# Attention with an expert layer: the large loads on ACT's queue, POOL's weight operations one period later

## The chip, the cores and the metric

The kernel runs on one core of a Trainium2 chip. The metric is device time in microseconds (us), the median of three runs; the times below, where nothing else is said, come from one execution that the hardware profiler recorded. The engines are TensorE (PE in the profile; PEld is its weight load), VectorE (DVE), ScalarE (ACT), GpSimd (POOL) and SyncE (SP). SP and ACT can each issue transfers (DMAs), and each has a queue of its own, which 16 DMA engines work off.

## The reference

Linear attention with exponential features over 8 batches and 8 heads, 576 positions of 64 numbers each, and then a two-layer expert network on the joined heads:

```python
def phi(x):
    proj = np.einsum('bhsd,df->bhsf', x, w_phi)              # 128 features
    proj = proj - np.max(np.abs(proj), axis=-1, keepdims=True)
    return np.concatenate([np.exp(proj), np.exp(-proj)], axis=-1)
q_p, k_p = phi(q), phi(k)
kv  = np.einsum('bhsf,bhsd->bhfd', k_p, v)
z   = np.sum(k_p, axis=2)
num = np.einsum('bhsf,bhfd->bhsd', q_p, kv)
den = np.einsum('bhsf,bhf->bhs', q_p, z)[..., None] + 1e-06
x   = (num / den) joined over heads                          # 4608 x 512
h   = x @ w_in                                               # w_in 512 x 2048
out = (h - np.tanh(h)) @ w_out                               # w_out 2048 x 512
```

The two expert weights arrive as 64-bit floats.

## The kernel before, in words

The work has two stages. The attention stage goes through 32 units, each a pair of heads of one batch, as a software pipeline: `ramp` starts the first three, `period(i)` for i from 3 to 31 works on six units at once, each at another step, and `drain` ends the last. The expert stage (`head`, `frame`, `finish`) then runs 48 frames of matmuls that take 7 products where a plain 2 x 2 block product takes 8. The order on each engine is the order in which the code is written; nothing is rescheduled. Each engine works its list in order and waits on semaphores for others.

In period i the names stand for units: `a` is unit i, `c` is i-1, `p` is i-2, `r` is i-3, `q` is i-4, `o` is i-5. A period does this:

- `project(a)`: PE projects the unit's queries and keys (tile `qk`) onto the features, into `pj`, `pa`, `pt`. `centre` on DVE finds the largest size in each row (`m`) and subtracts it (`t`). `k_exp` and `q_exp` on ACT take the exponentials (`kp`, `qe`).
- `kadd(c)`: POOL adds the key features of five blocks in four additions (L419 to L422) into `ss`. One period later `ksum` (L428) on PE sums `ss` over partitions, and `ksum_copy` (L432) on ACT copies the feature sums to `kst`.
- `denom(r)` on PE (L470) and `denom_copy` on ACT (L487) make the denominators `dd`. Then a chain of small transfers: `den_recip_load` (L492) gathers `dd` into `dn`; DVE takes the reciprocal `rn` (L497), ahead of the next period's `centre`; `den_store` (L502) writes it to memory as `rr`; in the next period `den_spread` (L507) reads it back spread over partitions as `rb`; in the period after that `den_mul` (L510) on POOL multiplies the attention output `d` with it, and `x_store` (L513) writes `d` to memory as `xs`.
- `kv` (L409), its copy, its transposition and `num` (L456) on PE make the numerators.
- Beside the attention, one tile of an expert weight per period is converted from 64 to 32 bits: `dec_load` (L267, L272) loads it raw (`rawi`, `rawo`), `dec_0` on ACT (L279) and three steps on DVE (L283 to L291) convert it. The converted tiles of `w_in` are combined in pairs for the 7 products: `Prep.steps` gives subtractions on POOL (L168, tiles `s` and the low parts of `wr`) and casts on ACT (L185, the high parts of `wr`). The table `aside` says in which period which of these run: `aside[i][0]` on ACT, `aside[i][1]` on POOL, `aside[i][2]` stores of finished pieces (`wd`, L112), `aside[i][3]` loads for the expert stage. A cast `h2` or `h4` stands one period after the POOL operation whose result it reads.
- `load(units[i+2])` (L303) fetches the queries and keys of the unit two periods on, 576 KB; `load_v` (L307) the values.

All loads and stores are issued by SP, except the first load of `w_phi`. On SP an instruction that waits holds up what is behind it.

Of the kernel before, what the change touches and what calls it, by code (L numbers as in the profile page):

```python
# [33 lines left out]
def tile_linear_attention_moe(  # L34
# [10 lines left out]
    nc = tc.nc  # L45
# [181 lines left out]
    with ExitStack() as c1:  # L227
# [32 lines left out]
        def dec_load(n, queue=nc.sync):  # L260
            u = Dec()
            kind, u.f = tiles[n]
            u.nm = f"{kind}{u.f}"
            u.d = wi if kind == "i" else wo
            u.r = raw.tile([P, DM], U64, tag="raw", name=f"raw{u.nm}")
            if kind == "i":
                queue.dma_start(  # L267
                    u.r.rearrange("p (c f) -> p c f", f=P),
                    w_in[:, u.f * P : (u.f + 1) * P].rearrange("(c p) f -> p c f", p=P),
                )  # L270
            else:
                queue.dma_start(u.r, w_out[u.f * P : (u.f + 1) * P, :])  # L272
            return u
# [26 lines left out]
        def load(u, queue=nc.sync):  # L300
            u.qk = pq.tile([P, PC], F32, tag="qk", name=f"qk{u.i}")
            for o, w in ((0, PC),) if u.i else ((5 * P, PC), (0, 5 * P)):
                queue.dma_start(u.qk[:, o:w], qkT[u.i][:, o:w])  # L303

        def load_v(u):
            u.v = pq.tile([P, 5, 2, D], F32, tag="v", name=f"v{u.i}")
            nc.sync.dma_start(u.v.rearrange("p j e d -> p (j e d)"), v5[u.i])  # L307


        def project(u, parts):  # L310
            for part in parts:
                if u.t is None:
                    u.t = [pq.tile([P, 2, 5, F], F32, tag="t0", name=f"t{u.i}_0"), None]
                    u.m = [p2.tile([P, 2, 5], F32, tag="m0", name=f"m{u.i}_0"), p2.tile([P, 2, 4], F32, tag="m1", name=f"m{u.i}_1")]
                if part == "j":
                    u.pj = ps_pj.tile([P, 2, 512], F32, tag="pj", name=f"pj{u.i}")
                    bank, tiles = u.pj, range(4)
                elif part == "t":
                    u.pt = ps_t.tile([P, 2, 512], F32, tag="pt", name=f"pt{u.i}")
                    bank, tiles = u.pt, range(4, 5)  # L320
                else:
                    u.pa = ps_d.tile([P, 2, 512], F32, tag="po", name=f"pa{u.i}")
                    bank, tiles = u.pa, range(5, 9)
                for k, a in enumerate(tiles):
                    for e in range(2):
                        hs = slice(e * D, (e + 1) * D)
                        nc.tensor.matmul(  # L327
                            bank[:, e, k * F : (k + 1) * F], u.qk[hs, a * P : (a + 1) * P], wph[hs, :], start=True, stop=True
                        )
# [10 lines left out]
        def centre(u, parts, h=None):  # L340
            for part in parts:
                x, m, t = part_of(u, part)
                if h is not None:
                    x, m, t = x[:, :, h], m[:, :, h], t[:, :, h]
                nc.vector.tensor_reduce(m, x, AX.X, ALU.max, apply_absolute_value=True)  # L345
                nc.vector.tensor_tensor(t, x, m.unsqueeze(3).broadcast_to(list(t.shape)), ALU.subtract)  # L346
# [48 lines left out]
        def k_exp(u, r, signs=(0, 1)):  # L395
            h, x, j = ((slice(SR, P), 4, 0), (slice(0, P), slice(0, 4), slice(1, 5)))[r]
            for s in signs:
                nc.scalar.activation(u.kp[h, :, j, s, :], u.t[r][h, :, x, :], AF.Exp, scale=1.0 - 2.0 * s)  # L398
# [18 lines left out]
        def kadd(u):  # L417
            x = p2.tile([P, 2, 2, F], F32, tag="ss", name=f"ss{u.i}")
            nc.gpsimd.tensor_tensor(x, u.kp[:, :, 1], u.kp[:, :, 2], ALU.add)  # L419
            nc.gpsimd.tensor_tensor(x, x, u.kp[:, :, 3], ALU.add)  # L420
            nc.gpsimd.tensor_tensor(x, x, u.kp[:, :, 4], ALU.add)
            nc.gpsimd.tensor_tensor(x, x, u.kp[:, :, 0], ALU.add)  # L422
            u.ss = x

        def ksum(u, x):
            u.pu = x
            for n in range(4):
                nc.tensor.matmul(x[n * 32 : (n + 1) * 32], ones, u.ss[:, n // 2, n % 2, :], start=True, stop=True)  # L428

        def ksum_copy(u):  # L430
            u.kst = p1.tile([P, F], F32, tag="kst", name=f"kst{u.i}")
            nc.scalar.copy(u.kst, u.pu)  # L432
# [31 lines left out]
        def denom(u, pu):  # L464
            u.pd = pu[:, F : F + CH]
            for s in range(2):
                for e in range(2):
                    for c in range(2):
                        n, w = 2 * e + c, 2 * e + s
                        nc.tensor.matmul(  # L470
                            u.pd[n * 32 : (n + 1) * 32, :],
                            u.ks[:, w * 32 : (w + 1) * 32],
                            u.qe[:, e, s, c * CH : (c + 1) * CH],
                            start=(s == 0),
                            stop=(s == 1),
                        )

        def num_copy(u):
            if u.i % 4 or u.i >= NU - 3:
                u.d = tail.tile([P, S], F32, tag="d", name=f"d{u.i}", bufs=3)  # L480
            else:
                u.d = p1.tile([P, S], F32, tag="d0", name=f"d{u.i}")
            nc.scalar.copy(u.d.rearrange("p (c n) -> p c n", c=2), u.po[:, :, 0:CH])  # L483

        def denom_copy(u):
            u.dd = pd.tile([P, CH], F32, tag="dd", name=f"dd{u.i}")
            nc.scalar.activation(u.dd, u.pd, AF.Identity, bias=bias_t[:, 3:4])  # L487

        def den_recip_load(u):
            w = 2 * S // P  # L490
            u.dn = tail.tile([P, w], F32, tag="dn", name=f"dn{u.i}")
            nc.sync.dma_start(u.dn, u.dd.rearrange("(n r) c -> n r c", r=32)[:, 0, :])  # L492
# [11 lines left out]
        def den_spread(u):  # L504
            u.rb = tail.tile([P, S], F32, tag="rb", name=f"rb{u.i}", bufs=1)
            for e in range(2):
                nc.sync.dma_start(u.rb[e * D : (e + 1) * D, :], u.rr[e : e + 1, :].broadcast_to([D, S]))  # L507

        def den_mul(u, pin=lambda ins: ins):
            pin(nc.gpsimd.tensor_tensor(u.d, u.d, u.rb, ALU.mult))  # L510

        def x_store(u):
            nc.sync.dma_start(xs[u.b // 2][u.hp, :, (u.b % 2) * S : (u.b % 2 + 1) * S], u.d)  # L513

        units = []
# [5 lines left out]
        NU = len(units)  # L521
# [7 lines left out]
        dec = []  # L529

        def unit(i):
            return units[i] if 0 <= i < NU else None

        def bank():
            return ps_c.tile([P, 512], F32, tag="pu", name="pu")
# [67 lines left out]
        def aside_at(i, late):  # L603
            for f in aside[i][late]:
                f()
# [56 lines left out]
        def period(i):  # L662
            a, c, p, r, q, o = (unit(i - n) for n in range(6))
            w = dec[i - 3]
            dec.append(dec_load(i - 2))
            if i > 3:
                num_copy(r)
            k_exp(c, 1)
            if o:
                den_mul(o)  # L670
                x_store(o)
            if i + 2 < NU:
                load(units[i + 2])
            project(a, "jat")
            centre(a, "jt")
            kadd(c)
            ksum(p, p.pc[:, 0:F])
            ksum_copy(p)
            pu = bank()
            denom(r, pu)  # L680
            denom_copy(r)
            den_recip_load(r)
            if q:
                den_spread(q)
            if i > 3:
                load_v(a)
            aside_at(i, 2)
            aside_at(i, 3)
            kv_turn(p)
            ksum_turn(p, p.pc[:, F : 2 * F])  # L690
            kv_turn_copy(p, nc.scalar.copy)
            ksum_turn_copy(p)
            dec_0(w, a.pt)
            if i < NU - 1:
                aside_at(i, False)
            aside_at(i, True)
            q_turn(c)
            q_turn_rest(c, pu)
            q_exp(c)
            q_exp_rest(c)  # L700
            centre(a, "a")
            k_exp(a, 0)
            kv(c)
            kv_copy(c)
            dec_1(w)
            dec_2(w)
            dec_3(w)
            if r:
                den_recip(r)
                den_store(r)  # L710
            num(p)
# [96 lines left out]
        for i in range(3, NU):  # L808
            period(i)
# [541 lines left out]
```

## Time and profile before

| | |
|---|---|
| three runs, median | 1057.58 us (1056.92 to 1059.92) |
| profiled execution, its own time | 1059.23 us |
| its span | 1057.4 us |
| PE busy | 1042.4 us (99%) |
| DVE busy | 870.2 us (82%) |
| ACT busy | 792.1 us (75%) |
| POOL busy | 272.8 us (26%) |
| bytes moved | 184.59 MB, 175 GB/s in the mean |

How to read it: PE counts as busy while any of its matmuls is under way, and their ends are modelled. A busy share over the whole span mixes the two stages: POOL has nearly all its work in the first 307 us. The granted clock of TensorE is full in all of both stages. The view by stretch tells the stages apart, the list of waits says who waited for whom, the chain follows the work that ended last, and the timeline shows when each instruction ran.

### The profile page before, as it was taken

The page shows a single profiled execution, that of the slowest core. Times are in us where ns is not written, and L with a number is a line of the kernel's source. Part 1 is how long each engine was busy: PE and PEld are TensorE (multiplying, and loading weights), DVE is VectorE, ACT ScalarE, POOL GpSimd, SP SyncE. Part 2 cuts the span into 40 slices and gives each one's busy share as a digit, 9 for nine tenths or more (in the row PEclk, how much of TensorE's full clock was granted, in tenths as well). Part 3 has the DMA queues.
Part 4 walks back from the last instruction along what each step waited for, and adds up shares of the span by engine and source line. Part 5 has one row for each costly group of instructions (what it writes and reads, how often), then busy time and mean ns, then how long its engine had stood idle before and what let it go on. Part 6 is the DMA issues. An engine that isn't in the chain of part 4 may idle for free.

```text
span 1057.4 us, 19349 instructions
## 1 busy us (share of the span) xinstructions
PE 1042.4 (99%) x7484; PEld 874.0 (83%) x7484; DVE 870.2 (82%) x1086; ACT 792.1 (75%) x1281; POOL 272.8 (26%) x233
## 2 busy tenths in 40 slices
PE   8999999999989999999999999999999999999998
PEld 6666666666668998999999999999999999999997
DVE  7899888889979899878887788867887778877776
ACT  5888888988878778766777666776677667776665
POOL 4799899989960000000000000000000000000000
PEclk9999999999999999999999999999999999999999
DMA  5789999999847653464335433345334543353311
GB/s 166 205 233 282 264 271 288 267 272 270 253 142 263 201 187 103 159 216 144 121 120 190 167 131 122 120 169 179 128 106 156 199 137 113 120 180 109 123 47 60
DMA packets 75738, 184.59 MB, mean 175 GB/s; under 512 B 15744, under 2 KB 30464, under 8 KB 75648
## 3 DMA queue, kind: packets, MB, share of 16 engines
q1 hardware_dynamic: 75360, 183.17, 53.9%
q8 instruction: 59, 0.97, 0.4%
q14 instruction: 31, 0.25, 0.1%
q10 hardware_dynamic: 288, 0.20, 0.1%
HBM read 149.49 MB, written 33.70 MB: 173 GB/s over the span
## 4 chain that ended last, share of the span: by engine, by line
PE 82%; DMA 7%; DVE 5%; ACT 2%; POOL 2%; issue 1%; SPq 1%; ACTq 0%; DVEq 0%; POOLq 0%
PE A L142 18%; PE B L142 14%; PE po L987 12%; PE po L988 12%; PE po L993 12%; DMA dn<-dd 4%; PE po L456 3%; PE pc L409 3%; DVE t L346 2%; PE pj L327 2%; PE pa L327 2%; PE pu L470 2%; DVE m L345 1%; DMA rb<-rr 1%; DMA rr<-rn 1%
## 5 line engine op out<-in xcount | busy, mean ns | idle before, releaser
L142 PE MATMUL A<-xo,wr 128*128 128x384 f32 x1152 | 231.5, 337 | 0.0
L142 PEld LDWEIGHTS A<-xo,wr 128*128 128x128 f32 x1152 | 204.9, 188 | 11.4 <-ACT d L483 0.5
L911 ACT COPY u<-A 128x384 f32<-128x384 f32 x143 | 68.5, 479 | 142.6 <-PE A L142 142.2
L142 PE MATMUL B<-xo,wr 128*128 128x384 f32 x864 | 173.7, 337 | 0.0
L142 PEld LDWEIGHTS B<-xo,wr 128*128 128x128 f32 x864 | 152.5, 188 | 4.2 <-DVE hx L918 0.4
L987 PE MATMUL po<-who,ghx 128*128 128x512 f32 x288 | 112.3, 390 | 0.7 <-ACT hy L925 0.7
L987 PE MATMUL po<-who,ghy 128*128 128x512 f32 x288 | 112.3, 390 | 0.3 <-ACT ghy L962 0.3
L988 PE MATMUL po<-wlo,ghx 128*128 128x512 f32 x288 | 112.0, 389 | 0.0
L988 PE MATMUL po<-wlo,ghy 128*128 128x512 f32 x288 | 112.0, 389 | 0.0
L510 POOL TENSOR_TENSOR d<-d,rb 128x576 f32<-128x576 f32 x32 | 46.3, 1448 | 165.4 <-DMA rb<-rr 160.8
L950 DVE SCALAR_TENSOR_TENSOR s2y<-s2y,thy 128x768 f32<-128x768 f32 x48 | 46.0, 959 | 51.5 <-ACT thy L941 51.5
L398 ACT ACTIVATE kp<-t 64x256 f32<-64x256 f32 (+1 forms) x126 | 85.1, 722 | 2.1 <-DVE t L346 1.0
L993 PE MATMUL po<-who,glx 128*128 128x512 f32 x288 | 80.9, 389 | 0.0
L935 ACT ACTIVATE yx<-hx 128x768 f32<-128x768 f32 (+1 forms) x49 | 41.0, 836 | 52.9 <-DVE hx L918 52.9
L993 PE MATMUL po<-who,gly 128*128 128x512 f32 x282 | 79.3, 389 | 0.3 <-DVE gly L965 0.3
L409 PE MATMUL pc<-kp,v 128*64 128x256 f32 x640 | 76.1, 384 | 0.5 <-DMA v<-in_v 0.4
L456 PE MATMUL po<-qe,kv 128*64 128x288 f32 x512 | 69.0, 412 | 0.4
L993 PEld LDWEIGHTS po<-who,glx 128*128 128x128 f32 x288 | 54.0, 188 | 11.2
L947 DVE SCALAR_TENSOR_TENSOR s2x<-s2x,yx 128x768 f32<-128x768 f32 (+1 forms) x49 | 46.1, 941 | 20.4 <-ACT s2x L936 19.1
L993 PEld LDWEIGHTS po<-who,gly 128*128 128x128 f32 x282 | 52.8, 188 | 11.7 <-DVE gly L965 0.8
L987 PEld LDWEIGHTS po<-who,ghx 128*128 128x128 f32 x288 | 54.1, 188 | 8.8 <-ACT hy L925 1.1
L987 PEld LDWEIGHTS po<-who,ghy 128*128 128x128 f32 x288 | 54.1, 188 | 8.5 <-ACT ghy L962 0.7
(186 smaller groups left out, 2228.8 us busy)
## 6 DMA issues: line engine op xcount, KB each, us to landing
wr<-wd SPq DMA_DIRECT2D x92, 512.0 KB
wr<-wd SPq DMA_DIRECT2D x46, 768.0 KB
qk<-in_qkT SPq DMA_DIRECT2D x31, 576.0 KB
v<-in_v SPq DMA_DIRECT2D x32, 320.0 KB
rb<-rr SPq DMA_DIRECT2D x64, 144.0 KB
xs<-d SPq DMA_DIRECT2D x32, 288.0 KB
out<-o SPq DMA_DIRECT2D x35, 256.0 KB
rawi<-in_moe_w_in SPq DMA_DIRECT2D x16, 512.0 KB
```

The costliest lines, as they stand in the source:

```text
L142: nc.tensor.matmul(bank[:, 0:HT], w[:, a, n, cs], x[:, b, c, :], start=start and i == 0, stop=i == 5, skip_group_check=not start,)
L327: nc.tensor.matmul(bank[:, e, k * F : (k + 1) * F], u.qk[hs, a * P : (a + 1) * P], wph[hs, :], start=True, stop=True)
L398: nc.scalar.activation(u.kp[h, :, j, s, :], u.t[r][h, :, x, :], AF.Exp, scale=1.0 - 2.0 * s)
L409: nc.tensor.matmul(u.pc[e * D : (e + 1) * D, 0 : 2 * F], u.v[:, j, e, :], u.kp[:, e, j, :, :], start=(j == first), stop=(j == last))
L456: nc.tensor.matmul(u.po[e * D : (e + 1) * D, c, 0:CH], u.kv[:, s, e * D : (e + 1) * D], u.qe[:, e, s, c * CH : (c + 1) * CH], start=(s == ...
L510: pin(nc.gpsimd.tensor_tensor(u.d, u.d, u.rb, ALU.mult))
L911: nc.scalar.copy(t, A[q][:, 0:HT])
L947: nc.vector.scalar_tensor_tensor(z.s[:, s], z.s[:, s], GC, z.y[:, s], ALU.add, ALU.mult)
L950: nc.vector.scalar_tensor_tensor(z.s[:, s], z.s[:, s], GK, z.th[:, s], ALU.mult, ALU.mult)
L987: nc.tensor.matmul(po, z.gh[:, ts], wh, start=first, stop=False)
L988: nc.tensor.matmul(po, z.gh[:, ts], wl, start=False, stop=False)
L993: nc.tensor.matmul(po, z.gl[:, ts], wh, start=False, stop=last)
```

## The change

Two things move, in `period` alone.

First, the raw weight load and the load of queries and keys are issued by ACT (`nc.scalar`) and stand behind `ksum_copy`; before, SP issued both, the first at the start of a period, the second behind `x_store`. Second, POOL does the weight operations of period i-1 in period i, between `den_mul` and `kadd`; before, it did those of period i at the end of period i, behind `kadd`. The last two periods keep their own weight operations at the end as well (there these are sums for the expert stage).

```diff
         def period(i):
             a, c, p, r, q, o = (unit(i - n) for n in range(6))
             w = dec[i - 3]
-            dec.append(dec_load(i - 2))
             if i > 3:
                 num_copy(r)
             k_exp(c, 1)
             if o:
                 den_mul(o)
                 x_store(o)
-            if i + 2 < NU:
-                load(units[i + 2])
+            if i <= NU - 2:
+                aside_at(i - 1, True)
             project(a, "jat")
             centre(a, "jt")
             kadd(c)
             ksum(p, p.pc[:, 0:F])
             ksum_copy(p)
+            dec.append(dec_load(i - 2, nc.scalar))
+            if i + 2 < NU:
+                load(units[i + 2], nc.scalar)
             pu = bank()
             denom(r, pu)
...
             if i < NU - 1:
                 aside_at(i, False)
-            aside_at(i, True)
+            if i >= NU - 2:
+                aside_at(i, True)
```

The next pieces show period 20, the one that starts at 182.14 us in the trace of the kernel before. On SP before, one period's transfers from the reciprocals' store on (`rawi` is a raw weight tile, `qk` the queries and keys of unit 22):

```order
L502 DMA rr_2765<-rn_2763 128x9
L267 DMA rawi_2776<-in_moe_w_in 128x4x128
L513 DMA xs_89<-d_2496 128x576
L303 DMA qk_2784<-in_qkT 128x1152
L492 DMA dn_2836<-dd_2834 128x1x9
L507 DMA rb_2838<-rr_2765 64x576 x2
L307 DMA v_2841<-in_v 128x640
L112 DMA wd_4_109<-wr_2_2430 128x512
L112 DMA wd_0_107<-wr_0_2571 128x512
```

The same on SP after:

```order
L502 DMA rr_2760<-rn_2758 128x9
L513 DMA xs_89<-d_2492 128x576
L492 DMA dn_2836<-dd_2834 128x1x9
L507 DMA rb_2838<-rr_2760 64x576 x2
L307 DMA v_2841<-in_v 128x640
L112 DMA wd_4_109<-wr_2_2430 128x512
L112 DMA wd_0_107<-wr_0_2571 128x512
```

The two large loads are gone from SP: the store of `xs` follows that of `rr`, and the gathering of `dn` follows `xs`. On ACT before, from the last exponentials to the first cast of a weight pair (`kst` are the feature sums, `dd` the denominators, `wr_1` the cast):

```order
L398 ACTIVATE kp_154<-t_1_2740 128x2x4x128 x2
L432 COPY kst_2823<-pc_2745 128x128
L487 ACTIVATE dd_2834<-pu,bias_t 128x288
L449 COPY kv_2848<-pc_2745 128x256
L441 COPY ks_2850<-pc_2745 128x128
L279 ACTIVATE pt_2807<-rawo_2635 128x512
L185 CAST wr_1_2853<-s_3_2711 128x512
```

The same on ACT after:

```order
L398 ACTIVATE kp_154<-t_1_2735 128x2x4x128 x2
L432 COPY kst_2819<-pc_2740 128x128
L267 DMA rawi_2821<-in_moe_w_in 128x4x128
L303 DMA qk_2823<-in_qkT 128x1152
L487 ACTIVATE dd_2834<-pu,bias_t 128x288
L449 COPY kv_2848<-pc_2740 128x256
L441 COPY ks_2850<-pc_2740 128x128
L279 ACTIVATE pt_2803<-rawo_2680 128x512
L185 CAST wr_1_2853<-s_3_2777 128x512
```

The two loads stand between the copy of the feature sums and that of the denominators. On POOL before, from the weight operations of period 19 (`s_3`, `s_4`) to those of period 20, with the multiplication `d` and the four additions `ss`:

```order
L168 TENSOR_TENSOR s_3_2711<-wi_2337 128x256
L168 TENSOR_TENSOR s_4_2712<-wi_2198,wi_2337 128x256
L168 TENSOR_TENSOR s_3_2711<-s_3_2711,wi_2198 128x256
L510 TENSOR_TENSOR d_2496<-d_2496,rb_2697 128x576
L419 TENSOR_TENSOR ss_2814<-kp_154 128x512
L420 TENSOR_TENSOR ss_2814<-ss_2814,kp_154 128x512
L421 TENSOR_TENSOR ss_2814<-ss_2814,kp_154 128x512
L422 TENSOR_TENSOR ss_2814<-ss_2814,kp_154 128x512
L168 TENSOR_TENSOR s_4_2712<-wi_2198,s_3_2711 128x256
L168 TENSOR_TENSOR wr_1_2853<-s_3_2711,wr_1_2853 128x512
```

The same on POOL after:

```order
L510 TENSOR_TENSOR d_2492<-d_2492,rb_2697 128x576
L168 TENSOR_TENSOR s_3_2777<-wi_2334 128x256
L168 TENSOR_TENSOR s_4_2778<-wi_2194,wi_2334 128x256
L168 TENSOR_TENSOR s_3_2777<-s_3_2777,wi_2194 128x256
L419 TENSOR_TENSOR ss_2810<-kp_154 128x512
L420 TENSOR_TENSOR ss_2810<-ss_2810,kp_154 128x512
L421 TENSOR_TENSOR ss_2810<-ss_2810,kp_154 128x512
L422 TENSOR_TENSOR ss_2810<-ss_2810,kp_154 128x512
L510 TENSOR_TENSOR d_2633<-d_2633,rb_2838 128x576
```

The three operations of period 19 have moved behind the multiplication of period 20 and ahead of its additions; the cast `wr_1` on ACT, which reads `s_3`, has kept its place in period 20.

## Rows read from the trace of the kernel before

**Rows 1.** By stretch: length, busy us (instructions) PE, PEld, DVE, ACT, POOL, clock, DMA, GB/s

```profile
42.12:284.19 242.07, 238.81 (x3044) 160.44 (x3043) 217.69 (x287) 212.69 (x418) 219.54 (x186) 1.00 0.90 264
284.19:306.60 22.41, 19.69 (x234) 11.95 (x232) 17.38 (x25) 17.44 (x32) 21.86 (x16) 1.00 0.58 191
340.00:1050.00 710.00, 710.00 (x3576) 644.04 (x3574) 569.22 (x688) 502.74 (x719) 6.06 (x3) 1.00 0.41 140
```

**Rows 2.** Timeline of period 20: start, us, engine, line, operation, tiles, [idle before]

```profile
182.14 1.16 PE L327 MATMUL pj<-wph,qk 64*128 64x128 f32 x16
...
183.00 0.75 POOL L168 TENSOR_TENSOR s<-s,wi 128x256 f32<-128x256 f32 x1
...
183.36 0.38 SPq L267 DMA_DIRECT2D rawi<-in_moe_w_in  x1
...
184.66 1.42 POOL L510 TENSOR_TENSOR d<-d,rb 128x576 f32<-128x576 f32 x1 [0.92 <-PE pt L327]
184.89 0.27 ACT L432 COPY kst<-pc 128x128 f32<-128x128 f32 x1
...
185.86 0.50 ACT L487 ACTIVATE dd<-pu,bias_t 128x288 f32<-128x288 f32 x1 [0.70 <-PE pu L470]
...
186.11 0.32 SPq L513 DMA_DIRECT2D xs<-d  x1
...
186.52 0.39 SPq L303 DMA_DIRECT2D qk<-in_qkT  x1
...
186.58 0.27 ACT L441 COPY ks<-pc 128x128 f32<-128x128 f32 x1
...
186.91 2.38 PE L409 MATMUL pc<-kp,v 128*64 128x256 f32 x20
187.00 0.59 SPq L492 DMA_DIRECT2D dn<-dd  x1
187.31 0.62 ACT L185 CAST wr<-s 128x512 fp32r<-128x512 f32 x1
...
187.69 1.14 SPq L507 DMA_DIRECT2D rb<-rr  x2
...
190.16 1.29 POOL L422 TENSOR_TENSOR ss<-ss,kp 128x512 f32<-128x512 f32 x1
...
191.23 1.16 PE L327 MATMUL pj<-wph,qk 64*128 64x128 f32 x16
...
193.44 0.43 PE L428 MATMUL pc<-ss,ones 128*32 128x128 f32 x8
```

**Rows 3.** Who waited for whom, 42.12 to 284.19 us: total, times, longest

```profile
POOL d L510 <- DMA rb<-rr: 11.7, 16, 1.8
...
DVE rn L497 <- DMA dn<-dd: 9.1, 11, 1.3
```

**Rows 4.** Chain that ended last, followed from 236 us: start, us, what

```profile
215.29 5.69 DMA dn<-dd
```

**Rows 5.** DMA queues, 2.5 to 3.3 us (q1 SP's, q10 ACT's): packets, MB, share

```profile
q1 hardware_dynamic: 118, 0.23, 73.9%
q10 hardware_dynamic: 122, 0.06, 29.9%
```

**Rows 6.** By stretch, POOL's weight operations (L168) alone

```profile
42.12:284.19 242.07, 51.34 (x56) 1.00 0.90 264
```

**Rows 7.** Timeline of POOL, the multiplications' first, latest and last

```profile
42.97 1.41 POOL L510 TENSOR_TENSOR d<-d,rb 128x576 f32<-128x576 f32 x1 [1.66 <-DMA rb<-rr]
...
212.97 1.41 POOL L510 TENSOR_TENSOR d<-d,rb 128x576 f32<-128x576 f32 x1 [1.75 <-DMA rb<-rr]
...
275.76 1.27 POOL L168 TENSOR_TENSOR wr<-wi,wr 128x512 fp32r<-128x512 f32 x1
277.68 1.41 POOL L510 TENSOR_TENSOR d<-d,rb 128x576 f32<-128x576 f32 x1 [0.65 <-DMA rb<-rr]
```

**Rows 8.** Line of the denominators' copy: ACT's sequencer waiting, ns least/median/most

```profile
L487 ACTq EVENT_SEMAPHORE  x31: 616/895/2111, 35.8 to 308.5; - x31
```

## The prediction

> **What bounds the kernel now.** I read the busy time by stretch first [rows 1]. In the expert stage, from 340 to 1050 us, TensorE has work all the time, and the change does not reach it. What can move is the attention stage: 26 whole periods from 42.12 to 284.19 us, and its end up to 306.6 us. A period with no stall lasts 9.09 us: the first projection of one starts at 182.14 us and of the next at 191.23 [rows 2]. The 26 periods took 242.07 us [rows 1], 9.31 each, so stalls cost them 242.07 - 26 x 9.09 = 5.7 us. That is the prize, 0.54% of the run.
>
> Next, who waits. DVE waited 11 times, 9.1 us in all, for `dn`, the gathered denominators, and POOL 16 times, 11.7 us, for `rb`, the spread reciprocals [rows 3]. The chain shows what the first does: `dn` is 5.69 us from issue to landing [rows 4]; the reciprocal follows on DVE, and in its order the row maxima of the next projection queue behind it. Both loads are small and stand behind large ones on SP's queue. In the period at 182 us [rows 2] the order is raw weight (183.36), `xs` (186.11, it waits for POOL's multiplication that began at 184.66 and took 1.42), `qk` (186.52), `dn` (187.00), `rb` (187.69). So there is a loop: multiplication, `xs`, `qk`, `dn`, `rb`, and the next period's multiplication.
>
> **The change part by part.** Times are sums against the profiled execution's 1059.23 us, which is its span of 1057.4 and 1.8 around it; the median of the three timed runs is 1057.58, and I move that by the same sum.
>
> (a) SP loses the two large loads. `dn` is issued 0.48 us after `qk` began to be issued [rows 2], and that goes out of the loop, so `dn` and `rb` start 0.48 earlier. Whether they also land sooner after their issue is open, since the same bytes still move at the same time, now from another queue. The DVE waits labelled with `dn` come to 9.1 us in 11 [rows 3]; 0.48 off each is 5.3, or 58%. I take the same share of the 5.7 us of stalls: -3.3. Bounds: 0 (the bytes in front are the same) and -5.7 (all stalls go).
>
> To set row against rule: during 0.8 us at the start both queues had work, and the engines took 118 packets (0.23 MB) from SP's and 122 (0.06 MB) from ACT's [rows 5]. They alternate one packet for one, whatever its size. The Trainium skill, page "DMA: Bandwidth & Descriptors", section "Queues, rings and completion order", says the same, and under "Issuing engines are not separate DMA queues" that a second issuing engine only saves the first one's issue time. By that rule the 0.48 is all there is, and (a) stays at -3.3; without it, small loads that overtake would give the whole -5.7. The row sides with the rule: a 2304-byte row of `rb` then alternates with a 4608-byte row of `qk`.
>
> (b) POOL puts the weight operations between the multiplication and the additions. They take 51.34 us in the 26 periods, 1.97 each [rows 6]. Now the additions end at 190.16 + 1.29 = 191.45, and TensorE wants them for the feature sums at 193.44: 1.99 us to spare, with a multiplication that began 2.52 into its period [rows 2]. With 1.97 more ahead of them the spare is 0.02. So from now on every delay of `rb` past that point is TensorE's. POOL waited 11.7 us for `rb` [rows 3], at the worst 1.75 us, ahead of the multiplication at 212.97 [rows 7]. Of the 26 multiplications the first starts at 42.97, 0.85 us into its period, the last at 277.68, 2.58 into the one that began at 284.19 - 9.09 = 275.10 [rows 1, 7]; read one by one they lie 0.84 to 3.54 us in, 2.68 in the mean. If none moves, the excess over 2.54 sums to 9 us; if all move forward by the 0.48 of (a), to 3. Some of that is the same lateness that (a) leaves, since a TensorE that waits here no longer waits there, so I take +2.1, with 0 and +9 as the ends.
>
> (c) ACT gets two issues a period behind the copy of the feature sums (184.89), ahead of the denominators' copy (185.86) [rows 2]. The cover is the wait for TensorE there: ACT's sequencer stood in it 895 ns in the median, 616 at the least [rows 8]. On SP the issues took 0.38 and 0.39 us, and the next began 0.41 to 0.48 after the last [rows 2]: about 0.95 for both. That is 0.05 over the median cover and 0.33 over the least. Queued behind is the chain denominators, `kv`, `ks`, and the first matmul after `ks` starts at 186.91, while `ks` ends at 186.58 + 0.27 = 186.85 [rows 2]: 0.06 of slack. So mostly nothing shows; I take 0.03 x 26 = +0.8. Bounds: 0 (ACT only gets work) and 0.33 x 26 = +8.6. No row shows a load's issue on ACT in this stage. The raw load starts 1.7 us later than now but is wanted a period later; `qk` is wanted two periods later, so the landings are covered.
>
> (d) One cast on ACT per even weight pair (187.31 in the period shown) reads what the third of POOL's weight operations wrote, at 183.00 for 0.75 us [rows 2]. Now all three come behind the multiplication: 184.66 - 0.48 + 1.42 + 3 x 0.75 = 187.85, so the cast waits 0.5. There are four such pairs; the exponentials behind it are wanted by TensorE only later, so I take half of 2.0: +1.0. Bounds 0, and 4 x 1.0 = +4 where `rb` is not earlier and the whole wait reaches TensorE.
>
> (e) At the end POOL bounds: from 284.19 to 306.60 it is busy for 21.86 of 22.41 us, and TensorE for 19.69 [rows 1]. The last weight operation (275.76, 1.27 us) ran ahead of the multiplication at 277.68, which then still waited 0.65 for `rb` [rows 7]; now it follows that multiplication. With `rb` 0.48 earlier the end moves by 1.27 - 0.48 = +0.8; bounds -0.65 (the wait goes) and +1.27.
>
> Sum: -3.3 + 2.1 + 0.8 + 1.0 + 0.8 = +1.4 us, so 1060.6 for the profiled execution and 1057.58 + 1.4 = 1059.0 for the median. The gain in one wait comes back as others.
>
> **Rivals.** First, faster: the small loads do overtake the large ones. For it: with fewer bytes ahead in their own queue `rb` need only beat 2.54 us into the period, and then POOL's multiplication can follow the additions at once. Against: one-for-one alternation [rows 5]. It gives -5.7 from (a), 0 from (b) and (d), +0.8 from (c) and 0 from (e): 1052.7.
>
> Second, slower: POOL's order decides. Place: the feature sums at 193.44 waiting for the additions. It decides once `rb` lands as late as now, so that the multiplication begins over 2.54 us into most periods. Price: (b) at +9, against which the whole wait of DVE is hidden (-5.7), with (c) +0.8, (d) +1 and (e) +1.3: +6.4, 1064.0. For it: the mean start of 2.68 is already past the point. Against: 0.48 of issue gone.
>
> Third, the loads do not fit on ACT: (c) at its upper end, +8.6 instead of +0.8, on the forecast's other terms: 1066.8. For it: 0.95 against 0.616 of cover; against: the median of 0.895.
>
> **How the numbers follow.** A measurement of this kernel tells 0.3%, 3.2 us, from no change, so faster means under 1054.4 and slower over 1060.8. Forecast 0.50, its own range 1055.5 to 1061.5, of which 0.42 lies within the bound and 0.08 above. First rival 0.25; second 0.19; third 0.06. Faster 0.25, same 0.42, slower 0.33. The range reaches to the first rival and past the second: 1052.5 to 1065.5, leaving out the third and the tail of the first.
>
> **What would show it.** Right: periods of about 9.25 us, fewer DVE waits for `dn`, a new wait of TensorE's feature sums for POOL's additions, the cast of (d) waiting for POOL, and the denominators' copy on ACT starting within 0.1 us of where it does. Wrong: multiplications that start under 1.5 us into the period (first rival); feature sums that wait over 0.3 us in most periods (second); the denominators' copy 0.3 us later in most periods (third). A larger wait in the expert stage would contradict all of it.

## The result, and the profile after

The changed kernel takes 1071.18 us (median of 4 runs, 1069.65 to 1072.38) against 1058.21 for the kernel before on the same chip: ratio 1.0121, 95% interval 1.0099 to 1.0143. It is slower by some 13 us, outside the range of the prediction and above all its rivals. The profiled execution took 1070.35 us, with a span of 1068.6.

First, where the 11.2 us of span lie. The table by stretch of the changed kernel answers to [rows 1] (length, busy us of PE, PEld, DVE, ACT, POOL, granted clock, DMA share, GB/s); the stretches are the same 26 periods, the end of the stage, and the expert stage:

```profile
42.80:294.90 252.10, 241.05 (x3046) 161.89 (x3044) 217.86 (x287) 211.05 (x418) 218.62 (x186) 1.00 0.87 255
...
294.90:317.20 22.30, 19.61 (x232) 11.88 (x232) 16.71 (x24) 17.46 (x32) 21.75 (x15) 1.00 0.57 179
...
345.00:1050.00 705.00, 705.00 (x3556) 640.40 (x3556) 565.44 (x683) 501.25 (x718) 5.95 (x3) 1.00 0.42 142
```

The 26 periods took 252.10 instead of 242.07 us, some 9.7 each instead of 9.31. That is 10.0 of the 11.2 us. TensorE stays fully busy in the expert stage, as it was. The granted clock is full in every row. DMA moved the same bytes at a lower share, 0.87 for 0.90: the engines had more empty time, not more work.

Second, who waited. The list of waits of the changed kernel in these periods, answering to [rows 3] (total us, times, longest):

```profile
POOL d L510 <- DMA rb<-rr: 28.1, 23, 3.1
DVE rn L497 <- DMA dn<-dd: 16.2, 18, 2.2
...
PE ptt L356 <- DVE t L346: 5.0, 6, 1.3
...
PEld pc L428 <- POOL ss L422: 4.1, 6, 1.2
...
PE pc L428 <- POOL ss L422: 2.8, 5, 1.1
...
PE pu L367 <- ACT dd L487: 1.9, 6, 0.4
...
ACT wr L185 <- POOL s L168: 1.3, 3, 0.5
```

The waits that the change was to shorten grew: `rb` from 11.7 us in 16 waits to 28.1 in 23, `dn` from 9.1 in 11 to 16.2 in 18. What TensorE itself lost stands in the rows that begin with PE: 5.0 us for the centred scores that DVE makes behind the late reciprocal (2.2 before), 2.8 for POOL's additions (none before), 1.9 for a transpose behind the denominators' copy (none before); together 9.7 us.

One late period shows the chain. This is the timeline of DVE and then of TensorE in the changed kernel (start, duration, engine, line, idle time ahead of it), in the period that starts at 159.4 us; `dn` had been issued at 154.60:

```profile
161.64 0.22 DVE L497 RECIPROCAL rn<-dn 128x9 f32<-128x9 f32 x1 [2.25 <-DMA dn<-dd]
161.77 1.16 DVE L345 TENSOR_REDUCE m<-pj 128x8 f32<-128x1024 f32 x1
162.96 1.23 DVE L346 TENSOR_TENSOR t<-pj,m 128x1024 f32<-128x1024 f32 x1
```

```profile
164.34 0.71 PE L356 MATMUL ptt<-ident,t 64*128 64x64 f32 x16 [0.88 <-DVE t L346]
```

DVE stood 2.25 us for `dn`; the row maxima of the next projection queue behind the reciprocal, and TensorE's transposes need their result.

Third, what moved on the queues. The timeline of the period that starts at 178.9 us, answering to [rows 2]:

```profile
181.08 1.42 POOL L510 TENSOR_TENSOR d<-d,rb 128x576 f32<-128x576 f32 x1 [0.72 <-DMA rb<-rr]
181.79 0.25 ACT L432 COPY kst<-pc 128x128 f32<-128x128 f32 x1
181.87 0.33 ACTq L272 DMA_DIRECT2D rawo<-in_moe_w_out  x1
182.25 1.23 ACTq L303 DMA_DIRECT2D qk<-in_qkT  x1
182.53 0.32 SPq L513 DMA_DIRECT2D xs<-d  x1
...
183.52 0.50 ACT L487 ACTIVATE dd<-pu,bias_t 128x288 f32<-128x288 f32 x1 [1.48 <-DVE t L346]
184.05 0.59 SPq L492 DMA_DIRECT2D dn<-dd  x1
```

The raw weight goes out 3.0 us into the period (1.2 in the period of [rows 2]), in one bunch with `qk` and `xs`. The issue of `qk` took 1.23 us of ACT here and held the denominators' copy to 4.6 us into the period (3.72 before). And the strip of the DMA engines (each digit the busy tenths of a fortieth of the stretch) shows what the bunch does. First two periods before, 182.14 to 200.32 us, then two of the changed kernel, 178.9 to 198.6:

```profile
DMA  5999998998899989899948999888999997987998
```

```profile
DMA  9999972094059999999999999950394899999999
```

Before, the 16 engines are evenly busy. In the changed kernel they run dry in stretches between 2.5 and 6 us into each of the two periods and are full for the rest, which is when `dn` and `rb` go. Laid over one another by the packets' own times, in the 26 periods, the busy share from 3 to 4 and from 4 to 5 us into the period fell from 0.83 and 0.92 to 0.43 and 0.63; from 6 to 9 us it rose from 0.91 to 1.00. Read one by one and averaged over the same 26 periods, `dn` takes 5.94 us from issue to landing instead of 5.06, and lands 10.91 us after the start of its period instead of 10.11.

### The profile page after: what moved, and what is told of

Its sections match the earlier page's. It is cut to its first block, busy times and chain, and to the rows that moved or that the text cites. A ratio compares the mean times of both kernels' runs of the same rounds, so it can differ in the third digit from the quotient of the medians.

```text
span 1068.6 us, 19312 instructions
## 1 busy us (share of the span) xinstructions
PE 1045.2 (98%) x7484; PEld 876.2 (82%) x7484; DVE 870.5 (81%) x1086; ACT 791.0 (74%) x1281; POOL 272.3 (25%) x233
## 4 chain that ended last, share of the span: by engine, by line
PE 73%; DMA 9%; ACT 6%; POOL 5%; DVE 3%; issue 2%; ACTq 1%; SPq 1%; POOLq 0%; DVEq 0%
PE A L142 18%; PE B L142 14%; PE po L990 12%; PE po L991 12%; PE po L996 12%; DMA rb<-rr 4%; DMA dn<-dd 3%; ACT kp L398 2%; PE pc L409 2%; PE po L456 1%; DMA xs<-d 1%; ACTq L303 1%; POOL d L510 1%; DVE t L346 1%; POOL ss L420 1%
## 5 line engine op out<-in xcount | busy, mean ns | idle before, releaser
L996 PEld LDWEIGHTS po<-who,glx 128*128 128x128 f32 x288 | 54.1, 188 | 11.2
L996 PEld LDWEIGHTS po<-who,gly 128*128 128x128 f32 x282 | 52.9, 188 | 11.6 <-DVE gly L968 0.7
L409 PEld LDWEIGHTS pc<-kp,v 128*64 128x64 f32 x640 | 43.1, 136 | 22.6 <-ACT ks L441 2.2
```

Of the source, the lines that this page charges most:

```text
L409: nc.tensor.matmul(u.pc[e * D : (e + 1) * D, 0 : 2 * F], u.v[:, j, e, :], u.kp[:, e, j, :, :], start=(j == first), stop=(j == last))
L996: nc.tensor.matmul(po, z.gl[:, ts], wh, start=False, stop=last)
```

## The experiments

All runs were timed against the kernel before on the same chip (medians from 1057.5 to 1059.3 us). "Period" is the mean of the 26 periods from some 42 us on; "raw" and "dn" are how far into its period the raw weight's load was issued and `dn` landed, in the mean.

| kernel | ratio to before (95%) | period | raw issued | dn landed |
|---|---|---|---|---|
| before | 1 | 9.31 | 1.90 | 10.11 |
| changed | 1.0121 (1.0099 to 1.0143) | 9.69 | 3.05 | 10.91 |
| loads on ACT only | 1.0075 (1.0049 to 1.0102) | 9.51 | 2.89 | 10.62 |
| POOL's order only | 1.0005 (0.9985 to 1.0025) | 9.40 | 1.75 | 10.00 |
| raw on ACT only | 1.0079 (1.0063 to 1.0094) | 9.53 | 3.02 | 10.76 |
| qk on ACT only | 0.9993 (0.9978 to 1.0009) | 9.24 | 1.62 | 9.90 |
| changed, raw back on SP | 1.0008 (0.9993 to 1.0022) | 9.21 | 1.52 | 9.80 |
| changed, loads on SP | 1.0245 (1.0229 to 1.0262) | 10.16 | 5.46 | 12.16 |
| loads on ACT, later | 1.0199 (1.0178 to 1.0219) | 10.13 | 4.66 | 11.80 |

**Half a change each.** First the two loads on ACT, with POOL's order as before:

```diff
-            dec.append(dec_load(i - 2))
...
-            if i + 2 < NU:
-                load(units[i + 2])
...
             ksum_copy(p)
+            dec.append(dec_load(i - 2, nc.scalar))
+            if i + 2 < NU:
+                load(units[i + 2], nc.scalar)
```

> Both large loads on ACT as in the change, POOL's order as before. Theory L (the loads are the loss: ACT's issues hold the denominators' copy, and the small transfers on SP take longer beside a second full queue): about 1068, 10 of the 13 us, dn 6 us from issue to landing. Theory P (POOL's order is the loss: the feature sums wait for the additions): about 1057, and dn as fast as before, 5 us. My prediction's own terms for this part alone: 1058.2 - 3.3 + 0.8 = 1055.7.

Then POOL's order alone, with the loads on SP:

```diff
+            if i <= NU - 2:
+                aside_at(i - 1, True)
             project(a, "jat")
...
-            aside_at(i, True)
+            if i >= NU - 2:
+                aside_at(i, True)
```

> Weight operations one period later on POOL, the loads on SP as before. Theory P: 1067 or more, the feature sums on TensorE waiting over 0.3 us in most periods. Theory L: 1058 to 1062, the wait for the additions replacing the waits of DVE for dn. By my prediction's upper end for this term: 1058.2 + 9 - 5.7 + 1 + 1.3 = 1063.8.

The loads alone: 1067.65 us, ratio 1.0075. POOL's order alone: 1060.43, ratio 1.0005, no change that can be measured. So most of the loss belongs to the loads. The two together lose more (1.21%) than the two apart add up to (0.80%), though the intervals leave little room between them. With the loads alone, TensorE's new wait is that for the scores behind the reciprocal, here from that run's waits (2.2 us in 5 before):

```profile
PE ptt L356 <- DVE t L346: 6.9, 9, 1.3
```

**ACT's time for issuing.** Two loads of 1 KB issued by ACT at the place of the change, all else as before:

```diff
             ksum_copy(p)
+            for n in range(2):
+                nc.scalar.dma_start(tiny[n], w_phi2[:, 0:2])
```

> The kernel before, plus two loads of 1 KB each per period that ACT issues at the place where the change has its large loads; the loads read nothing that is used. It prices ACT's issues without their bytes. If the issues themselves are the loss: 1062 or more, with the denominators' copy 0.3 us or more later. If the loss comes from the bytes behind them: 1058 to 1060, with that copy 0.1 us later at most.

It took 1071.06 us, ratio 1.011 (1.0079 to 1.0142), but this is not the price of two ordinary issues. Three of the 26 periods took 12.5 to 12.7 us. This is what happened in the first of them (lines from 251 on are one higher in this kernel):

```profile
45.71 2.65 ACTq L681 DMA_DIRECT2D tiny<-in_w_phi  x2
48.47 0.50 ACT L488 ACTIVATE dd<-pu,bias_t 128x288 f32<-128x288 f32 x1 [2.57 <-PE ptt L357]
49.02 0.33 PE L368 MATMUL pu<-ident,t 64*128 64x64 f32 x2 [1.43 <-ACT dd L488]
49.45 4.07 PE L410 MATMUL pc<-kp,v 128*64 128x256 f32 x20
```

The second issue alone took 2.23 us, the denominators' copy came late, TensorE stood 1.43 us for it, and then the granted clock of TensorE fell to the lower of its two levels for a while: it averages 0.59 from 49.40 to 53.55 us, and the twenty `kv` matmuls took 4.07 us instead of 2.38 [rows 2]. In the second such period an issue took 2.43 us, with the same result; in the third DVE stood 2.65 us for `dn`, and TensorE then 1.70 for the scores. Over each of the three the granted clock averages 0.86 or 0.87. Of the 52 issues 42 took under 0.40 us, and the other 23 periods average 9.30 us, as before (9.31). So short issues cost nothing that shows, and a long one can cost over 3 us. Why an issue of 1 KB takes over 2 us is open.

**Small loads ahead of qk.** The kernel before, with `qk` behind `rb` on SP:

```diff
             if q:
                 den_spread(q)
+            if i + 2 < NU:
+                load(units[i + 2])
             if i > 3:
                 load_v(a)
```

> The kernel before, with the load of queries and keys still on SP but behind the spread reciprocals: the small loads go ahead of the 576 KB in the same queue. If dn and rb were late because of what stands ahead of them in one queue, dn lands 1 us sooner after its issue and the run is 1053 to 1055. If the engines are simply full and the order in a queue tells little, it stays at 1058.

1066.34 us, ratio 1.0061 (1.0042 to 1.0081), neither of the two times expected. `dn` now takes 3.34 us from issue to landing (5.06 before), and the multiplications start 1.3 us into the period. But another load pays. From this run's waits, TensorE's first and then SP's:

```profile
PE pc L409 <- DMA v<-in_v: 8.5, 10, 1.7
```

```profile
SPq L507 <- DMA rr<-rn: 35.2, 20, 2.9
```

SP holds `rb` until `rr` has landed, and `v`, queued behind, comes late. One period of 12.34 us makes 3.0 of the 6.4 us that the 26 periods lose: TensorE stood 1.56 us for `v` there, and the granted clock averages 0.86 over that period. So what stands ahead of `dn` in SP's queue does set its time, and a gain for one load is a loss for the next.

**Queue or place.** The changed kernel with both loads issued by SP, at the changed place in the program:

```diff
-            dec.append(dec_load(i - 2, nc.scalar))
+            dec.append(dec_load(i - 2))
             if i + 2 < NU:
-                load(units[i + 2], nc.scalar)
+                load(units[i + 2])
```

> The changed kernel with both large loads issued by SP again, but at the changed kernel's place in the program (behind the feature sums' copy, that is behind xs and ahead of dn). Arrival theory: the loss comes from raw and qk being on the engines together, right ahead of dn; so it stays without ACT: dn is 5.9 us or more from issue to landing, time 1064 to 1072. Issue theory: the loss comes from ACT's time for issuing, ahead of the denominators' copy; so that copy is back at 3.72 to 3.9 us into the period and the time within 0.3% of before, 1057 to 1062.

1083.34 us, ratio 1.0245: the worst of all, without a single load on ACT. Its timeline of SP shows why, in the period that starts at 194.8 us:

```profile
199.55 0.32 SPq L513 DMA_DIRECT2D xs<-d  x1
199.97 0.39 SPq L267 DMA_DIRECT2D rawi<-in_moe_w_in  x1
200.44 0.53 SPq L303 DMA_DIRECT2D qk<-in_qkT  x1
201.07 0.60 SPq L492 DMA_DIRECT2D dn<-dd  x1
```

Both loads wait behind `xs`, which waits for POOL, so raw goes out 5.2 us into the period. Neither theory had put it there: `dn` takes 5.33 us from issue to landing, not 5.9, but it is issued only 6.83 us into the period, behind both loads. So ACT's queue is not needed for a loss. Against this kernel it even helped, since there the loads need not wait for POOL.

**Which load.** Only the raw weight on ACT, `qk` on SP as before:

> The kernel before with only the raw weight's load moved to ACT behind the feature sums' copy; qk stays on SP. Arrival theory: raw now arrives with xs, qk and dn instead of ahead of them, so xs takes over 5 us and dn over 5.5 instead of 3.8 and 5.1; time 1061 to 1066. Issue theory: one issue of 0.35 to 0.5 us lies under the wait for the denominators (616 ns at the least), so nothing is lost: 1057 to 1061, the denominators' copy at 3.72 us.

Only `qk` on ACT, raw on SP as before:

> The kernel before with only qk's load moved to ACT behind the feature sums' copy, 1.0 us earlier than SP issued it. Idle-engines theory: engines stay evenly busy, dn is issued 0.4 us earlier and lands no later after its issue; 1054 to 1059. Rival (small loads lose against a second queue): xs and dn take 0.5 to 1 us longer each, 1061 to 1065.

Raw alone: 1065.86 us, ratio 1.0079, the whole loss of both loads. `qk` alone: 1057.04, ratio 0.9993, nothing. The time of raw alone is the one that the arrival theory gave, but not its reason: `xs` takes 4.1 us from issue to landing and `dn` 5.18 (3.7 and 5.06 before), not over 5 and 5.5. `dn` is issued later instead, 5.58 us into the period for 5.06, behind a later `xs`. The denominators' copy is at its old place but for a few periods (3.77 us in the mean for 3.74), so ACT's time is not what costs there; the waits for `dn` grew all the same (9.1 us in 11 before):

```profile
DVE rn L497 <- DMA dn<-dd: 14.4, 13, 2.2
```

With raw early and `qk` on ACT, `xs` takes 6.1 us instead of 3.7 and nothing is lost: a slower `xs` costs nothing by itself.

The strip of the DMA engines for raw alone, two periods from 173.9 to 193.6 us, has no such hole as the changed kernel's:

```profile
DMA  8779899998889898785999799999679999979987
```

From 2 to 6 us into the period the engines are 0.82 busy in the mean of the 26 periods (0.88 before, 0.69 in the changed kernel). With `qk` alone on ACT, which loses nothing, it is 0.81.

**Raw back at its place.** The changed kernel with one line moved back:

```diff
             w = dec[i - 3]
+            dec.append(dec_load(i - 2))
...
             ksum_copy(p)
-            dec.append(dec_load(i - 2, nc.scalar))
             if i + 2 < NU:
                 load(units[i + 2], nc.scalar)
```

> The changed kernel with only the raw weight's load put back on SP at the head of the period, 1.2 us in; qk stays on ACT, POOL's order as changed. Idle-engines theory: with raw 1.7 us later the 16 DMA engines have too little to move from 3 to 5 us into the period (0.43 and 0.62 busy in the changed kernel, 0.83 and 0.92 before) and are full from 6 us on, when dn and rb go; with raw early the dip goes, dn is back at 5.2 us or less and the time at 1058 to 1062. Rival (ACT and POOL have no slack for this): one issue on ACT and POOL's order keep the loss, 1065 to 1071.

1058.66 us, ratio 1.0008: the loss is gone, with `qk` on ACT and POOL's new order still there. The waits of the 26 periods of this run, and the strip of the DMA engines from 181.6 to 200.1 us:

```profile
POOL d L510 <- DMA rb<-rr: 12.3, 15, 3.1
...
DVE rn L497 <- DMA dn<-dd: 6.2, 12, 0.9
...
PE pc L428 <- POOL ss L422: 0.9, 2, 0.6
```

```profile
DMA  7799989899897899998688998988999946899999
```

The deep hole is gone (0.81 busy from 2 to 6 us). `dn` lands at 9.80 us because it is issued early, at 4.39; from there it takes 5.41 us, no less than before. TensorE's waits for POOL fell to 0.9 us. ACT's issues are also short again. The line of `qk`'s load in the changed kernel and in this one (ns least, median, most):

```profile
L303 ACTq DMA_DIRECT2D qk<-in_qkT x27: 334/463/1257, 27.0 to 279.1; - x27
```

```profile
L303 ACTq DMA_DIRECT2D qk<-in_qkT x27: 334/334/342, 27.0 to 267.4; - x27
```

**The loads on ACT, but later.** Both loads on ACT behind the copy of the summed keys, 1.8 us later than with the loads alone:

> Both large loads on ACT as in the changed kernel, but some 1.5 us later, behind the copies of kv and of the summed keys (ks); POOL as before. Arrival theory: dn is issued ahead of both loads, so it lands 4.0 us or less after its issue, the reciprocal stands under 1.1 us into the next period, and the time is 1053 to 1060. Issue theory: ACT pays the same two issues, 0.9 us, ahead of the query exponentials, so the first kv matmul of the unit or the row maxima are late and the time stays at 1063 to 1070.

1078.99 us, ratio 1.0199. My theory of arrival, that it is enough to issue `dn` ahead of the two loads, was not tested: in 23 of 25 periods raw still went out ahead of `dn`, since SP came to `dn` late too (5.68 us into the period), and `dn` took 6.1 us. Raw goes out 4.66 us into the period, the DMA engines are 0.44 and 0.38 busy from 4 to 5 and from 5 to 6 us, and everything that follows is late. Over the kernels of the table the loss goes with the time at which raw is issued.

**Another load in the hole.** The changed kernel with `v` at the head of the period, where raw stood:

> The changed kernel (raw and qk on ACT, late; POOL's order as changed) with only the load of v moved on SP from behind rb to the head of the period, where raw stood before the change. Idle-engines theory: 320 KB at the head fill most of the hole that the late raw left from 3 to 5 us into the period, and leave less to move when dn and rb go; over half of the loss of 12.8 us goes, 1057 to 1064. Rival (what costs is raw's own lateness, or ACT's two issues): raw and the issues stand where they stood, so 1067 to 1073.

1067.43 us, ratio 1.0089 (1.0064 to 1.0113): the expectation of the idle-engines theory missed, and the number lies where the rival put it. But the run does not separate the two, since the hole was not filled. The strip from 175.6 to 194.5 us:

```profile
DMA  9999952077789899999999999794879479969999
```

It only moved forward: the busy share is now lowest, 0.45 and 0.51, from 2 to 4 us into the period. My reading is that `v` no longer stands at the end of the period, where it kept the engines busy while SP waits for the reciprocal. The next kernel has the same hole without a late raw: the kernel before with raw, `v`, `qk`, `xs`, `dn`, `rb` in this order on SP.

> The kernel before, all loads on SP, with every large load ahead of the small ones: raw, v, qk, xs, dn, rb. Idle-engines theory: the engines have work from 2 to 5 us and the small loads follow in an emptier queue, so dn falls to 4.5 us or less: 1053 to 1057. Rival (v between raw and qk only pushes qk, xs and dn back by its 320 KB): dn 5.5 us or more, 1058 to 1064.

1064.04 us, ratio 1.0059 (1.0036 to 1.0082): the idle-engines theory missed a second time, and `dn`, at 6.01 us, is where the rival had it. Without `v` behind `rb` the engines drain (0.44 and 0.49 from 2 to 4 us), and `dn` lands at 10.70. So here is a loss with raw early and a deep hole, and above, with raw alone late, a loss without one. From its list, SP's wait ahead of the store of `rr` (52.9 us in 25 before):

```profile
SPq L502 <- DVE rn L497: 81.2, 26, 4.7
```

**The semaphores.** Each transfer signals its landing on one of eight semaphores, which are handed out in turn, so a transfer can come to wait for the last one on its own. In the kernels with raw late, the store of `rr` was sometimes held after the reciprocal: 0.33 us in the mean and 2.84 at most in the changed kernel, 0.03 before. In the longest case a store of `wd` (L112) ahead of it on SP stood until `xs`, which has the same semaphore, had landed at 143.07 us. From the list of SP's waits in the changed kernel:

```profile
SPq L112 <- DMA xs<-d: 14.3, 6, 4.6
```

Two kernels were to take such sharing away by writing the store of `xs` down behind the two loads, with every engine's own order unchanged:

```diff
             if o:
                 den_mul(o)
-                x_store(o)
...
                 load(units[i + 2], nc.scalar)
+            if o:
+                x_store(o)
```

> The changed kernel with every engine's order as it is; only the line that writes down the store of xs stands behind the two loads in the program. The eight completion semaphores are handed out in the program's order, so the store of rr, eight DMAs on, now shares one with raw instead of xs and no longer waits for xs to land (in the changed kernel rr was issued 0.33 us after the reciprocal in the mean, at most 2.84, in the kernel before 0.03). Semaphore theory: those waits are a large part of the loss, rr follows the reciprocal at once, 1060 to 1066. Idle-engines theory: the late raw alone lengthens xs and dn; rr follows at once, but the time stays at 1067 to 1072.

> Both large loads on ACT, POOL as before, and the store of xs written down behind the two loads, so that rr shares its completion semaphore with raw and not with xs. Semaphore theory: the loss of the two loads alone (0.75%) goes, 1056 to 1061. Idle-engines theory: it stays, 1063 to 1068.

The changed kernel so altered: 1071.59 us, ratio 1.0141 (1.0123 to 1.0159); the one with POOL as before: 1066.07, ratio 1.0083 (1.0070 to 1.0096). But in their traces each of the 496 transfers that SP and ACT issue has the place and the semaphore that it had without the edit. So the sharing was not changed, and the two are repeats: they bear out the loss of the whole change and that of the loads alone. They do show that the time does not follow the hold: with the loads alone it was 0.23 us in the mean in the traced execution of 1065.78 us, and 0.05 in that of the repeat, 1068.25. Without one period of 12.53 us in the repeat, with the granted clock low in a part of it, the periods average 9.50 us against 9.51.

**Looking for a faster order.** Three orders of SP's loads were tried for speed. `dn`, `v`, `rb`, `qk` behind `xs`:

> The kernel before, all loads on SP, with its order changed to raw, xs, dn, v, rb, qk (before: raw, xs, qk, dn, rb, v). Arrival theory: nothing large stands ahead of dn, so dn takes 3.3 to 4.0 us as when qk alone went behind rb, and v is in time because it no longer stands behind qk; periods near 9.1 us, time 1052.5 to 1056. Rival: the stage's bytes just fit, so one of rb (behind v) or qk comes late in its turn and TensorE waits for it: 1058 or more.

1061.12 us, ratio 1.0039 (1.0024 to 1.0053), where the arrival theory had 1052.5 to 1056. `dn` takes only 2.9 us, but `rr` 5.7 (3.9 before), since `qk` now stands ahead of it; the multiplications start 4.4 us into the period, and TensorE waits for POOL's additions, 8.3 us in 10 waits. Then raw, `qk`, `xs`, `dn`, `rb`, `v`, without and with POOL's new order:

> The kernel before, all loads on SP, with qk ahead of xs (raw, qk, xs, dn, rb, v instead of raw, xs, qk, dn, rb, v): qk goes out some 2 us earlier, as soon as the projections have read its buffer, and not behind POOL's multiplication. Idle-engines theory: the engines are filled at 2 to 4 us into the period and less loaded when dn and rb go, dn falls under 4.5 us, periods come near 9.1 us, 1052.5 to 1056. Rival (the order in SP's queue is all): dn still stands behind qk and xs, latency 5 us or more, 1057 to 1060.

> The order of loads raw, qk, xs, dn, rb, v on SP, and POOL's new order of the change beside it. Idle-engines theory: with rb earlier the multiplication starts before 2.5 us into nearly every period, so POOL's new order costs nothing: within 1.5 us of the same order of loads with POOL as before. Rival (POOL has no spare in any case): feature sums wait for POOL's additions in over a third of the periods, 4 us or more above it.

The first has the shortest periods of all, 9.19 us. By stretch, 26 of them:

```profile
42.10:281.00 238.90, 237.54 (x3044) 160.04 (x3042) 217.78 (x286) 211.87 (x418) 220.10 (x187) 1.00 0.89 268
```

Its time, 1056.16 us, ratio 0.9993 (0.9980 to 1.0006), can't be told from that of the kernel before, and `dn` still takes 5.06 us, not under the 4.5 of the idle-engines theory. With POOL's new order it is 1058.33, ratio 1.0009 (0.9995 to 1.0024): 2.2 us more where at most 1.5 was expected, but the intervals overlap. No kernel here is shown to beat the kernel before.

## Why the prediction was wrong

**The step that failed** is a sentence in (c): "The raw load starts 1.7 us later than now but is wanted a period later; `qk` is wanted two periods later, so the landings are covered." Its first half is right: no list of waits of the changed kernel names raw. But I priced the later load by its own user alone, and gave it nothing. That load is 512 of the some 2500 KB of a period, on engines that are busy 0.90 of the time. It went out 1.15 us later in the mean (1.90 to 3.05). With only this load moved the kernel loses 0.79%, 8.4 us (6.7 to 9.9), and `dn` lands 0.65 us later in its period; with only this load moved back the whole change costs 0.08%. The 0.75% of the two loads alone is 7.9 us (5.2 to 10.8); the sum had -2.5 for them, (a) and (c) together.

**(a)** had the wrong sign for the same reason. Its lower bound, 0, rested on "the bytes in front are the same". They were not: raw used to be issued 2.2 us ahead of `xs` in the mean (1.90 against 4.12) and now is 1.2 us ahead of it, in one bunch with `qk`. `dn` was issued at 4.97 instead of 5.06 us into the period, so even the 0.48 us of issue did not come through: `xs` goes out later, and the denominators' copy too. With raw back on SP, `dn` is issued at 4.39 and the wait for `dn` is 6.2 us for 9.1, so the issue moves as (a) had it; but the -3.3 us does not show there either: `qk` alone on ACT gives -0.7 us (-2.3 to +1.0). The rule of the Trainium skill that (a) leaned on, page "DMA: Bandwidth & Descriptors", section "Issuing engines are not separate DMA queues", agrees with that run: 0.9993, no gain beyond issue time. It speaks of who issues; the load that cost here was one that went out later.

**(b)** was right in its mechanism and its cover, though its excess over 2.54 us, added up again, is 8.4 us and not 9. POOL's order alone costs 0.05% (interval -0.15 to 0.25), within its bounds of 0 to 9 us, and with raw early the complete rest of the change costs 0.08% (0.8 us), near the +1.4 of the sum. With raw late the spare of 0.02 us is overdrawn: TensorE waits 2.8 us for POOL. From the loads alone to the changed kernel the ratio rises by a further 0.46% (their intervals just meet), and by 0.58% between the repeats of the two (1.0083 and 1.0141, intervals apart); POOL's waits and ACT's long issues are both in it, and no run parts them.

**(c)**, the issues themselves: 0.33 for raw was as expected, `qk` took 0.46 in the median but up to 1.26. The denominators' copy starts 3.96 us into the period in the median for 3.72, over 0.3 us late in 12 of 26: the sign named for the third rival, short of most. TensorE's wait for it is 1.9 us, the size of the term rather than of its upper end.

**(d)** held: three casts waited 1.3 us in all for POOL. **(e)** held: from the end of the 26 periods to the first matmul of the expert stage it is 23.4 us (294.83 to 318.22) for 22.8 before (284.19 to 306.96), +0.6 for +0.8.

**The rivals.** The first did not happen: the multiplications start 2.8 us into the period, not under 1.5. The second's sign, a wait of over 0.3 us, is in 3 periods of 26. None of them had the raw load's place in it, so none gave 1071.

**What stays open.** That the move of the raw load decides is shown: the loss comes with it alone and goes when it alone goes back. That its time decides, and not its queue, is likely and not isolated: both loads still later on ACT lose more (1.99% for 0.75%), and late on SP they lose 2.45%, but no kernel issued raw early from ACT. How it acts is open. The hole in the engines' work is plain in the changed kernel, but it does not tell losers from the others: raw alone, `qk` alone and the changed kernel with raw back have the engines 0.82, 0.81 and 0.81 busy from 2 to 6 us, and only the first loses. What raw alone shows is a later `dn` (issued at 5.58 for 5.06) rather than a slower one (5.18 us for 5.06); with both loads late `dn` is slower (5.83 us with the loads alone, 5.94 in the changed kernel). Other paths are out: no user waits for raw, ACT's time for issuing is not needed (with raw alone the denominators' copy keeps its place but for a few periods), and the time does not follow the hold of `rr`.

## What to carry to other kernels

Where the DMA engines are near full, do not price a moved load at nothing because its own user still gets it in time. Ask also whose transfers it then goes out with, and whether a loop of small transfers, here `xs`, `dn`, `rb` and the multiplication, gets longer by it. The strip of the DMA engines over one period shows a hole at a glance, but count the hole against a kernel that did not lose before calling it the cause. And split a change of two parts before explaining it: here one line of it carried most of the loss.

## What the hardware did that was not expected

ACT's issue of a 576 KB load took 334 to 342 ns in all 27 cases where no other load had been issued by ACT just ahead, but up to 1257 ns right behind a 512 KB one. Of 52 issues of a 1 KB load on ACT, two took over 2.2 us, and no wait that the trace names explains them. And a stall of TensorE cost more than its length: three times in that run TensorE stood 1.4 to 1.7 us, the granted clock then fell, and the twenty `kv` matmuls behind the first of these stalls took 4.07 us instead of 2.38.
